# A first FFN block of 256 tokens with attention woven into it, in windowed attention followed by a SwiGLU block

## The chip, the cores and the metric

The kernel runs on one core of a Trainium2 chip. A core has a matrix engine (PE, with its weight loads listed apart as PEld), a vector engine (DVE), a scalar engine (ACT), a general engine (POOL) and a sync engine (SP). Each of the five executes its own instructions in order and waits for the others by semaphores. POOL and SP also issue transfers (DMAs). PE writes only to PSUM, which ACT and DVE then read ("evict") into SBUF. The metric is the device time of one execution in microseconds (us); smaller is better.

## The reference

Attention over 4 batches, 8 heads, 768 tokens and 64 dimensions per head. A token sees the first 4 tokens (the sinks) and the last 128 tokens up to itself. The heads of a token side by side form a row of 512, and 3072 such rows go through a SwiGLU feed-forward block of width 1536.

```python
scores = scale * np.matmul(q, k.transpose(0, 1, 3, 2))
is_sink = pos[None, :] < 4
rel = pos[:, None] - pos[None, :]
in_window = (rel >= 0) & (rel < 128)
a = softmax(np.where(is_sink | in_window, scores, -1e9))
x = (a @ v).transpose(0, 2, 1, 3).reshape(B * S, H * D)
g = x @ w_gate
out = (g * sigmoid(g) * (x @ w_val)) @ w_out
```

## The kernel before

**Groups.** Attention works in 12 groups of 256 tokens, three per batch. Group g needs its own values and the last 128 of the group before it; groups 0, 3, 6 and 9 open a batch and have no earlier window. Its steps are:

- *T* (`step_T`): k and q arrive with tokens in the partitions, and PE transposes them so that the head dimension is there. Each batch has two parts (`PARTS`): part 0 holds its first 512 tokens and takes four T steps, part 1 holds the other 256 and takes two. One step makes eight transposes into one PSUM tile `pt` of the pool `ps_a`, half of it (h = 0) evicted by ACT (L257), the other half (h = 1) by DVE (L259), four copies of 64x256 each, all into one SBUF tile `kqT` per batch.
- *S* (`step_S`, four per group, one per pair of heads): matmuls of scores into `s` (L282, the pool `ps_s` with one buffer), one exp on ACT (L287), one product with the 0/1 mask on DVE (L291).
- *K* (`step_K`): scores against the sinks, for groups that do not open a batch.
- *PV* (`step_PV`, four per group): probabilities times values, with a column of ones for the sum; DVE takes the reciprocal (L331) and scales (L332).
- *X* (`step_X`, two per group): transposes the 128 rows and copies them (L353) into `xT`, the input of an FFN block.

**FFN blocks.** The 3072 rows are cut into blocks, `SIZES = [512, 256, 512, 512, 512, 512, 256]`. A block has 12 gate units (one for 128 columns of the width: four matmuls `pg`, tanh on ACT, four matmuls `pv`, then u and ht on DVE, L386 to L399) and one down unit per 128 rows (12 matmuls `pd`, an ACT copy, a store over SP, L412 to L419). `pg`, `pv` and `pd` share the pool `ps_f` with three buffers.

**Order.** It is written out by hand. `weave(us, slots)` runs the units one after another and hands each unit the attention steps of its slot; a gate unit runs them between `pg` and `pv`. What a step leaves for DVE goes into the list `later`, and `flush()` at the end of the unit emits it, behind the unit's own u and ht. The evictions of T are not put off in this way: they are emitted inside the step, so ahead of u. `pro` runs steps without FFN and emits one put-off item at a time. Before the first gate, T of part 0 and all of groups 0 and 1 run through `pro`. Then come nine gates of block 0 (512 tokens: groups 0 and 1), then T of part 1 and all of group 2 alone (`alone`, slot 9), then nine gates of block 1 (256 tokens: group 2), the other gates of both, and six down units with groups 3 and 4 in the slots. Blocks 2, 3 and 4 hold two groups each by `pair`, blocks 5 and 6 hold group 11.

**Loads.** Nearly all go through POOL's queue, which converts to bf16, in the order of the program: half of the first k and q (two loads of 256 KB), the builds of the identity, of `diag_h` and of the masks on POOL itself, the other half, values of groups 0 and 1 (eight loads each), weights of gate pieces 0 to 3 (`FCH`: the 12 gate units come in pieces of 1, 2, 3, 3 and 3), part 1 of batch 0, and so on. SP loads only `vcf`, the values of the sinks (eight small loads), from which DVE makes `vsb` for all four batches before its first eviction (L205).

Of the kernel before, what the change touches and what calls it, by code (L numbers as in the profile page):

```python
# [15 lines left out]
def kernel(  # L16
# [26 lines left out]
    SIZES = [512, 256, 512, 512, 512, 512, 256]  # L43
# [43 lines left out]
    def load_kq(b, a, k2):  # L87

        t0, r = PARTS[a]
        if k2 == 0:  # L90
            nat[b, a] = natp.tile([P, 2, H, r * D], BF16, tag=f"kq{a}", name="kq")
        hs = slice(4 * k2, 4 * k2 + 4)
        for i, src in ((0, k), (1, q)):
            nc.gpsimd.dma_start(
                nat[b, a][:, i, hs],
                src[b, hs, t0:t0 + r * P].rearrange("h (p r) d -> p h (r d)", r=r))

    def load_v(g):
        b, c = divmod(g, GC)
        va = vpool.tile([P, 2, H, VS], BF16, tag=f"va{g}", name="va")  # L100
        nc.vector.memset(va[:, :, :, D:D + 1], 1.0)
        for j in range(2):
            t0 = c * 256 + j * P
            for r in range(4):
                nc.gpsimd.dma_start(  # L105
                    va[32 * r:32 * (r + 1), j, :, 0:D],
                    v[b, :, t0 + r:t0 + P:4].rearrange("h m d -> m h d"))
        vas[g] = va
# [27 lines left out]

    nc.vector.memset(vcf, 0.0)
    nc.vector.memset(vcf[:, :, D:D + 1], 1.0)
    for h in range(H):
        nc.sync.dma_start(  # L140
            vcf[h * NS:(h + 1) * NS, :, 0:D],
            v[:, h, 0:NS].rearrange("b s d -> s b d"))

    load_kq(0, 0, 0)
    make_identity(nc, ident)
    nc.gpsimd.memset(diag_h, 1.0)
# [8 lines left out]
    def build_masks():  # L155
        nc.gpsimd.memset(mask, 1.0)
        for w in range(4):
            m = mask[32 * w:32 * (w + 1)].rearrange(
                "p a (k r m) -> p a k r m", k=2, r=4)
            nc.gpsimd.affine_select(  # L160
                out=m[:, :, 0], in_=m[:, :, 0], compare_op=ALU.is_gt, fill=0.0,
                base=w, pattern=[[0, 2], [-1, 4], [-4, 32]], channel_multiplier=4)
            nc.gpsimd.affine_select(
                out=m[:, :, 1], in_=m[:, :, 1], compare_op=ALU.is_ge, fill=0.0,
                base=-w, pattern=[[0, 2], [1, 4], [4, 32]], channel_multiplier=-4)

        nc.gpsimd.tensor_copy(out=mask0, in_=mask)
        for w in range(4):
            nc.gpsimd.memset(
                mask0[32 * w:32 * w + 1].rearrange("p a x -> p (a x)")[:, P:3 * P], 1.0)  # L170

    load_kq(0, 0, 1)
    build_masks()
    load_v(0)
    load_v(1)
    for i in range(4):
        load_gate(i)

    def load_b(b):
        for k2 in range(2):  # L180
            load_kq(b, 1, k2)
# [4 lines left out]

    load_b(0)
    load_v(2)
    load_gate(4)
    load_a(1)  # L190
    for i in range(4):
        load_out(i)
    load_v(3)
# [9 lines left out]
    for b in range(B):  # L203
# [7 lines left out]


    kqT, es_t, e_t, xns, xTs = {}, {}, {}, {}, {}
# [7 lines left out]
    def step_T(b, a, n):  # L221
        t0, r = PARTS[a]
        if a == 0 and n == 0:
            kqT[b] = kqtp.tile([P, NP2, 2, S], BF16, tag="kqT", name="kqT")
        ns = r // 2
        pairs = range(n * 2 // ns, (n + 1) * 2 // ns)
        pt = ps_a.tile([P, 2, 4, P], BF16, tag="a", name="pt")
        for h in range(2):
            m = 0
            for p in pairs:  # L230
                for i in range(2):
                    for x in range(ns):
                        nc.tensor.transpose(  # L233
                            pt[:, h, m],
                            nat[b, a][:, i, 2 * p + h, 2 * x * D:2 * (x + 1) * D],
                            ident)
                        m += 1
        for h in range(2):
            for u in range(2):

                src = pt[u * D:(u + 1) * D, h]
                dst = kqT[b][h * D:(h + 1) * D, pairs[0]:pairs[-1] + 1]
                dst = dst.rearrange("q a i s -> q (a i) s")[:, :, t0:t0 + r * P]
                if r == 4:
                    dst = dst.rearrange("q i (t x u m) -> q i x t u m", t=4, x=2, u=2)
                    src = src.rearrange("q (i x) (t m) -> q i x t m", x=2, t=4)
                    for i in range(2):
                        evict(h, dst[:, i, :, :, u], src[:, i])
                else:
                    dst = dst.rearrange("q i (t w u m) -> q i t w u m", t=2, w=2, u=2)  # L250
                    src = src.rearrange("q i (t m w) -> q i t w m", t=2, w=2)
                    for w in range(2):
                        evict(h, dst[:, :, :, w, u], src[:, :, :, w])

    def evict(h, dst, src):
        if h == 0:
            nc.scalar.copy(out=dst, in_=src)  # L257
        else:
            nc.vector.tensor_copy(out=dst, in_=src)  # L259

    def step_ks(b):

        dst = kss[b].rearrange("q (a m) -> q a m", m=KS)
        for h in range(2):
            r = slice(h * D, (h + 1) * D)
            nc.vector.tensor_copy(
                out=dst[r, :, h * NS:(h + 1) * NS], in_=kqT[b][r, :, 0, 0:P:P // NS])

    def step_S(g, p):
# [3 lines left out]
        ps = ps_s.tile([P, 2, 512], FP32, tag="s", name="s")  # L273
        kT, qT = kqT[b][:, p, 0], kqT[b][:, p, 1]
# [4 lines left out]
        for kk, qq, n, col in parts:  # L279
            for h in range(2):  # L280
                r = slice(h * D, (h + 1) * D)
                nc.tensor.matmul(  # L282
                    ps[:, h, col:col + n], kT[r, kk:kk + P], qT[r, qq:qq + n],
# [270 lines left out]
```

## Time and profile before

| | |
|---|---|
| median of 3 runs | 308.81 us (308.06 to 309.0) |
| the profiled execution | 307.91 us, its span 306.2 us |
| PE busy | 258.8 us of the span (85%) |
| DVE busy | 198.2 us (65%) |
| ACT busy | 135.6 us (44%) |
| POOL busy | 98.4 us (32%) |

The profile is of one execution; times in it count from the start of its span. A row of the timeline has the start, the length, the engine, the line of the kernel, the operation, and out<-in with shapes; xN means that N instructions in a row are merged, and the bracket tells how long the engine stood idle before and what ended that. A row of the groups has the busy time and the mean length in ns, and behind the second bar the idle time before them. A row of the waits has the total in us, how often, and the longest. The busy time of PE overstates its work, since matmuls are pipelined.

### The profile page before, as it was taken

To read this page: it belongs to the slowest core of one execution; us is meant where nothing else is said; L and a number is where in the kernel's file an instruction comes from. 1 tells how busy PE (TensorE), PEld (TensorE's weight loads), DVE (VectorE), ACT (ScalarE), POOL (GpSimd) and SP (SyncE) were. 2 spreads that over 40 slices of the span, in tenths; PEclk is the share of its full clock that TensorE was granted. 3 is DMA by queue.
4 is the path that set the end of the run, shared out by engine and by line. 5 is a ranking of instruction groups with operands and counts; after the bars stand their busy time and mean duration, and the time that the engine had idled before them with its cause. 6 is when DMAs were issued, how large, how long until landed. Compare 5 with 4: busy or idle time off the path is not lost.

```text
span 306.2 us, 5085 instructions
## 1 busy us (share of the span) xinstructions
PE 258.8 (85%) x1920; PEld 140.0 (46%) x1920; DVE 198.2 (65%) x462; ACT 135.6 (44%) x261; POOL 98.4 (32%) x165
## 2 busy tenths in 40 slices
PE   0357896588799988889997897999999999999980
PEld 0235443366444543454543444544555445566430
DVE  2766678576876348699546697918997278977000
ACT  1572235526835255844156446436554263333220
POOL 8999376369877244690000000000000000000000
PEclk9999999599999999999999799999999999999996
DMA  7399999999999598692120000022000220000122
GB/s 98 47 58 135 196 111 198 205 83 103 132 79 113 88 158 112 44 102 16 39 81 22 0 2 0 4 70 67 1 0 2 67 72 1 2 0 1 42 89 77
DMA packets 53240, 20.81 MB, mean 68 GB/s; under 512 B 36320, under 2 KB 50144, under 8 KB 53216
## 3 DMA queue, kind: packets, MB, share of 16 engines
q0 software_dynamic: 49888, 14.16, 44.7%
q1 hardware_dynamic: 3328, 6.32, 6.7%
q8 instruction: 15, 0.25, 0.3%
q14 instruction: 9, 0.07, 0.1%
HBM read 28.34 MB, written 6.29 MB: 113 GB/s over the span
## 4 chain that ended last, share of the span: by engine, by line
PE 65%; DVE 16%; ACT 10%; issue 3%; DMA 1%; SPq 1%; DVEq 0%; ACTq 0%
PE pd L412 20%; PE pv L394 16%; PE pg L386 16%; DVE kqT L259 6%; PE s L282 5%; DVE u L398 4%; ACT e L287 4%; ACT kqT L257 4%; PE o L326 4%; PE pt L233 2%; ACT th L389 2%; PE px L350 2%; DVE ht L399 1%; DMA vcf<-in_v_dram 1%; DVE e L291 1%
## 5 line engine op out<-in xcount | busy, mean ns | idle before, releaser
L394 PE MATMUL pv<-xT,wv 128*128 128x512 bf16 (+1 forms) x336 | 76.8, 351 | 10.4 <-DVE u L398 8.5
L389 ACT ACTIVATE th<-pg 128x512 f32<-128x512 f32 (+1 forms) x84 | 45.1, 536 | 87.6 <-PE pg L386 79.2
L386 PE MATMUL pg<-xT,wg 128*128 128x512 bf16 (+1 forms) x336 | 76.8, 351 | 1.6 <-DVE xT L353 1.0
L412 PE MATMUL pd<-wo,ht 128*128 128x512 bf16 x288 | 68.3, 379 | 0.4 <-DVE ht L399 0.4
L398 DVE SCALAR_TENSOR_TENSOR u<-th,pg 128x512 bf16<-128x512 f32 (+1 forms) x84 | 51.2, 610 | 23.7 <-ACT th L389 22.3
L105 POOL DMA_DIRECT2D va<-in_v_dram x96 | 55.8, 619 | 33.1 <-DMA kq<-in_q_dram 11.5
L399 DVE TENSOR_TENSOR ht<-u,pv 128x512 bf16<-128x512 bf16 (+1 forms) x84 | 51.4, 612 | 9.5 <-PE pv L394 1.0
L287 ACT ACTIVATE e<-s 128x1024 bf16<-128x1024 f32 (+1 forms) x48 | 45.6, 950 | 13.2 <-PE s L282 13.0
L386 PEld LDWEIGHTS <-wg 128*128 128x128 bf16 x336 | 32.9, 98 | 33.3 <-issue 3.5
L394 PEld LDWEIGHTS <-wv 128*128 128x128 bf16 x336 | 30.5, 97 | 34.5 <-issue 16.4
L259 DVE COPY kqT<-pt 64x256 bf16<-64x256 bf16 x96 | 27.9, 330 | 19.7 <-ACT kqT L257 16.7
L412 PEld LDWEIGHTS <-ht 128*128 128x128 bf16 x288 | 26.2, 98 | 27.5 <-issue 1.0
L291 DVE TENSOR_TENSOR e<-e,mask 128x1024 bf16<-128x1024 bf16 (+1 forms) x48 | 30.8, 642 | 11.0 <-ACT e L287 10.8
L257 ACT COPY kqT<-pt 64x256 bf16<-64x256 bf16 x96 | 30.5, 367 | 15.9 <-PE pt L233 15.4
L416 ACT ACTIVATE ot<-pd 128x512 f32<-128x512 f32 x24 | 14.3, 597 | 44.3 <-PE pd L412 44.2
L282 PE MATMUL s<-kqT 64*128 64x128 bf16 (+1 forms) x256 | 21.0, 263 | 15.4 <-ACT e L287 10.4
L233 PE MATMUL pt<-ident,kq 128*128 128x128 bf16 x192 | 16.2, 234 | 9.2 <-DMA kq<-in_k_dram 5.9
L282 PEld LDWEIGHTS <-kqT 64*128 64x128 bf16 x256 | 9.4, 100 | 30.5 <-issue 24.1
L326 PEld LDWEIGHTS <-e 128*128 128x128 bf16 x352 | 19.3, 107 | 7.4 <-DVE xn L332 0.8
L332 DVE TENSOR_TENSOR xn<-o,rcp 128x256 bf16<-128x256 f32 x48 | 20.4, 424 | 1.7
L326 PE MATMUL o<-va,e 128*128 128x65 bf16 x352 | 20.9, 207 | 0.7 <-DVE xn L332 0.7
L233 PEld LDWEIGHTS <-kq 128*128 128x128 bf16 x192 | 13.0, 105 | 12.7 <-DMA kq<-in_k_dram 5.9
(35 smaller groups left out, 115.3 us busy)
## 6 DMA issues: line engine op xcount, KB each, us to landing
out_dram<-ot SPq DMA_DIRECT2D x24, 256.0 KB
va<-in_v_dram POOLq DMA_DIRECT2D x96, 32.0 KB, 2.6
kq<-in_k_dram POOLq DMA_DIRECT2D x8, 256.0 KB, 7.1
kq<-in_q_dram POOLq DMA_DIRECT2D x8, 256.0 KB, 8.0
wo<-in_moe_w_out_dram POOLq DMA_DIRECT2D x4, 384.0 KB, 12.6
wg<-in_moe_w_gate_dram POOLq DMA_DIRECT2D x3, 384.0 KB, 7.4
wv<-in_moe_w_val_dram POOLq DMA_DIRECT2D x3, 384.0 KB, 8.6
kq<-in_k_dram POOLq DMA_DIRECT2D x8, 128.0 KB, 3.7
```

What stands on the lines that cost most here:

```text
L105: nc.gpsimd.dma_start(va[32 * r:32 * (r + 1), j, :, 0:D], v[b, :, t0 + r:t0 + P:4].rearrange("h m d -> m h d"))
L257: nc.scalar.copy(out=dst, in_=src)
L259: nc.vector.tensor_copy(out=dst, in_=src)
L282: nc.tensor.matmul(ps[:, h, col:col + n], kT[r, kk:kk + P], qT[r, qq:qq + n], start=True, stop=True)
L287: nc.scalar.activation(e, ps[:, :, lo:512], AF.Exp, scale=scale)
L326: nc.tensor.matmul(o, l, r, start=(i == 0), stop=(i == len(mms) - 1), skip_group_check=True)
L386: nc.tensor.matmul(pg, wgs[fi][:, c, fs], x[:, c, 0:n], start=(c == 0), stop=(c == DMC - 1))
L389: nc.scalar.activation(th, pg, AF.Tanh, scale=0.5)
L394: nc.tensor.matmul(pv, wvs[fi][:, c, fs], x[:, c, 0:n], start=(c == 0), stop=(c == DMC - 1))
L398: nc.vector.scalar_tensor_tensor(u, th, 1.0, pg, op0=ALU.add, op1=ALU.mult)
L399: nc.vector.tensor_tensor(hts[tb][:, f, 0:n], u, pv, op=ALU.mult)
L412: nc.tensor.matmul(po, hts[tb][:, f, ts * P:(ts + 1) * P], wos[f // n][:, f % n], start=(f == 0), stop=(f == DFC - 1))
```

## The change

Five things change together.

1. The blocks become `[256, 512, 512, 512, 512, 512, 256]`. Only group 0 runs ahead of the first gate. Groups 1 and 2, the T steps of part 1 and K of both go into the slots of block 0, which has 14 units; groups 3 and 4 with T of batch 1 go into block 1 by `pair(3, 4, 2)`. Ahead of the first gate every second S step (`wide`) uses two tiles of `ps_f` and two exps, so that it need not wait for `s`.
2. A T step now serves one head of two pairs (part 0) or of four pairs (part 1). K lies in one half of `pt` and is evicted by ACT into a tile `kT`; Q lies in the other and is evicted by DVE into a tile `qT`; two copies of 64x512 each. Within the FFN the Q copies go into `later`, so behind u and ht.
3. The values of group 0 are loaded in fp32 over SP, ahead of `vcf`, into two tiles of the output pool, and DVE casts them (`cast_v`).
4. The masks are built by DVE compares from two index tiles that POOL makes (`iota`); the identity and `diag_h` are cleared by DVE. `vsb` of a batch is made after its fourth T step.
5. The loads on POOL are reordered: weights of gate pieces 0 and 1 come right behind the first k and q, and w_out ahead of batch 1. A load of part 1 covers all heads and half the partitions, with a token order that lets the eviction read without a stride.

```diff
-    SIZES = [512, 256, 512, 512, 512, 512, 256]
+    SIZES = [256, 512, 512, 512, 512, 512, 256]
...
+            else:
+                for w in range(2):
+                    nc.gpsimd.dma_start(
+                        nat[b, a][64 * w:64 * (w + 1), i],
+                        src[b, :, t0:t0 + r * P].rearrange(
+                            "h (n w u) d -> w n h (u d)", w=2, u=2)[w])
...
+    v32 = [opool.tile([P, DM], FP32, tag="ot", name="v32") for _ in range(2)]
+    for j in range(2):
+        for r in range(4):
+            nc.sync.dma_start(
+                v32[j][32 * r:32 * (r + 1)].rearrange("p (h d) -> p h d", d=D),
+                v_src(0, j, r))
...
+    nc.gpsimd.iota(tq, [[1, 4], [4, 32]], base=0, channel_multiplier=0,
+                   allow_small_or_imprecise_dtypes=True)
+    for w in range(4):
+        nc.gpsimd.iota(tk[32 * w:32 * (w + 1)], [[0, 1]], base=w,
+                       channel_multiplier=4, allow_small_or_imprecise_dtypes=True)
...
+        for j in range(2):
+            nc.vector.tensor_scalar(mask[:, j, 0:P], tq, tk, None, op0=ALU.is_lt)
+            nc.vector.tensor_scalar(mask[:, j, P:2 * P], tq, tk, None, op0=ALU.is_ge)
...
-    load_kq(0, 0, 1)
-    build_masks()
-    load_v(0)
-    load_v(1)
-    for i in range(4):
-        load_gate(i)
+    va0 = new_v(0)
+    load_gate(0)
+    load_gate(1)
+    load_v(1)
+    load_gate(2)
+    load_kq(0, 1, 0)
+    load_gate(3)
+    load_gate(4)
+    load_v(2)
...
+        def evict(i):
+            dst = (kTs if i == 0 else qTs)[b][
+                h * D:(h + 1) * D, pairs[0]:pairs[-1] + 1, t0:t0 + r * P].rearrange(
+                "q a (x u m) -> q a x u m", u=2, m=32)
             for u in range(2):
+                d = dst[:, :, :, u]
+                src = pt[u * D:(u + 1) * D, i].rearrange(
+                    "q (a x m) -> q a x m", a=len(pairs), m=32)
+                if i == 0:
+                    nc.scalar.copy(out=d, in_=src)
                 else:
+                    nc.vector.tensor_copy(out=d, in_=src)
+        evict(0)
+        if now:
+            evict(1)
         else:
+            later.append(lambda: evict(1))
...
+                later.append(lambda: build_vsb(b))
...
+    T0, S0, V0, X0 = Ta(0, True), Ss(0), PVs(0), Xs(0)
+    pro(T0[0], T0[1], S0[0], A(step_S, 0, 1, True), T0[2], T0[3], S0[2],
+        A(step_S, 0, 3, True), cast_v)
     flush()
+    pro(*V0)
+    flush()
+    pro(*X0)
     flush()
...
+    v1, x1, v2, x2 = PVs(1), Xs(1), PVs(2), Xs(2)
+    add(sl, *zip((0, 1, 2, 3), Ss(1)), (1, A(step_K, 1)), (4, v1[0]), (4, v1[1]),
+        (5, v1[2]), (5, v1[3]), *zip((5, 6), Tb(0)), *zip((6, 7), x1),
+        *zip((7, 8, 9, 10), Ss(2)), (8, A(step_K, 2)), (11, v2[0]), (11, v2[1]),
+        (12, v2[2]), (12, v2[3]), (12, x2[0]), (13, x2[1]))
+    weave(units(0), sl)
...
+    sl = pair(3, 4, 2)
+    for i, t in zip((0, 1, 2, 3), Ta(1)):
+        sl.setdefault(i, []).insert(0, t)
+    weave(units(1), sl)
```

More of the change, by code (lines that the diff above doesn't have):

```diff
@@ L219, in flush, with step_T @@
         later.clear()
[L221 removed]
+    def step_T(b, a, n, now):
         t0, r = PARTS[a]
         if a == 0 and n == 0:
[L224 to L238, printed above, removed]
[L239 to L253 removed]
```

150 lines of the change are left out of this document (72 added, 78 removed).

## The prediction

> **What bounds the kernel now.** I read the windows first, cut where the FFN blocks begin, then the start, then the waits of the later blocks.
>
> ```profile
> span 306.2 us, 5085 instructions
> 0.00:33.30 33.30, 15.71 (x153) 11.00 (x154) 20.13 (x64) 13.93 (x26) 29.90 (x56) 1.00 0.85 93
> 33.30:48.90 15.60, 15.60 (x74) 7.09 (x74) 11.12 (x17) 5.38 (x9) 10.63 (x17) 1.00 1.32 156
> 48.90:63.90 15.00, 8.19 (x89) 5.70 (x88) 10.29 (x25) 6.97 (x13) 5.45 (x9) 0.66 1.40 192
> 63.90:109.20 45.30, 41.84 (x345) 24.86 (x345) 28.94 (x78) 21.70 (x45) 33.35 (x54) 1.00 0.96 97
> 109.20:155.40 46.20, 41.50 (x314) 21.37 (x312) 33.66 (x79) 23.65 (x49) 19.07 (x31) 1.00 0.66 78
> 155.40:205.10 49.70, 44.55 (x338) 22.98 (x336) 33.91 (x78) 25.16 (x50) 0.00 (x0) 0.97 0.07 21
> 205.10:244.40 39.30, 39.05 (x282) 18.94 (x280) 28.90 (x60) 18.93 (x33) 0.00 (x0) 1.00 0.10 28
> 244.40:306.20 61.80, 52.34 (x336) 28.09 (x334) 31.29 (x62) 19.89 (x36) 0.00 (x0) 0.96 0.11 36
> ```
>
> Columns: stretch, its length, busy PE, PEld, DVE, ACT, POOL, then clock, DMA share, GB/s. PE is the bound wherever FFN runs: 15.60 of 15.60 in the first gates, 39.05 of 39.30 in block 4. It isn't in two stretches of attention alone: up to 33.30 (15.71 busy) and 48.90 to 63.90 (8.19 of 15.00, at clock 0.66). Blocks 2 and 3 lose 4.7 and 5.15 us.
>
> The start:
>
> ```profile
> 7.41 1.68 PE L233 MATMUL pt<-ident,kq 128*128 128x128 bf16 x14 [1.12 <-DMA kq<-in_q_dram]
> 7.85 3.24 DVE L205 TENSOR_TENSOR vsb<-vcf,diag_h 128x520 bf16<-128x520 f32 x4 [4.94 <-DMA vcf<-in_v_dram]
> ...
> 15.26 0.50 PE L282 MATMUL s<-kqT 64*128 64x256 bf16 x4 [1.11 <-ACT e L287]
> ...
> 16.76 1.28 ACT L257 COPY kqT<-pt 64x256 bf16<-64x256 bf16 x4 [0.16 <-PE pt L233]
> 17.20 1.03 PE L233 MATMUL pt<-ident,kq 128*128 128x128 bf16 x8
> 18.08 1.00 DVE L259 COPY kqT<-pt 64x256 bf16<-64x256 bf16 x4 [2.15 <-ACT kqT L257]
> ...
> 33.28 1.02 PE L386 MATMUL pg<-xT,wg 128*128 128x512 bf16 x4 [0.52 <-DVE xT L353]
> ```
>
> The first q lands at 7.4, the first gate starts at 33.28: 25.9 us for attention of groups 0 and 1. DVE's evictions begin behind 3.24 us of vsb, and always when ACT's four copies of the same pt are over (16.76 + 1.28, then 18.08).
>
> The later blocks:
>
> ```profile
> PE pv L394 <- DVE u L398: 8.5, 8, 2.1
> ```
> ```profile
> 111.92 1.53 DVE L259 COPY kqT<-pt 64x256 bf16<-64x256 bf16 x4 [3.10 <-ACT kqT L257]
> ...
> 113.46 0.69 DVE L398 SCALAR_TENSOR_TENSOR u<-th,pg 128x512 bf16<-128x512 f32 x1
> 114.20 1.02 PE L394 MATMUL pv<-xT,wv 128*128 128x512 bf16 x4 [1.51 <-DVE u L398]
> ```
> ```profile
> 119.48 0.68 DVE L291 TENSOR_TENSOR e<-e,mask 128x1024 bf16<-128x1024 bf16 x1
> 119.90 1.02 ACT L287 ACTIVATE e<-s 128x1024 bf16<-128x1024 f32 x1
> ```
>
> DVE is in order. Its copy waits for ACT's, u waits behind that copy, pv finds no free PSUM buffer and PE stands: 8.5 us over the kernel.
>
> **The change, part by part.** Durations that I use:
>
> ```profile
> L353 DVE COPY xT<-px 128x512 bf16<-128x512 bf16 x24 | 10.0, 419 | 8.1 <-PE px L350 8.1
> L398 DVE SCALAR_TENSOR_TENSOR u<-th,pg 128x256 bf16<-128x256 f32 x24 | 10.1, 421 | 3.2 <-ACT th L389 3.2
> L399 DVE TENSOR_TENSOR ht<-u,pv 128x256 bf16<-128x256 bf16 x24 | 10.1, 421 | 2.5
> L291 DVE TENSOR_TENSOR e<-e,mask 128x1024 bf16<-128x1024 bf16 x32 | 22.0, 687 | 9.8 <-ACT e L287 9.7
> L291 DVE TENSOR_TENSOR e<-e,mask 128x768 bf16<-128x768 bf16 x16 | 8.9, 553 | 1.2 <-ACT e L287 1.2
> L332 DVE TENSOR_TENSOR xn<-o,rcp 128x256 bf16<-128x256 f32 x48 | 20.4, 424 | 1.7
> L331 DVE RECIPROCAL rcp<-o 128x4 f32<-128x4 f32 x48 | 8.5, 177 | 4.4 <-PE o L326 4.0
> ```
> ```profile
> L416 ACT ACTIVATE ot<-pd 128x512 f32<-128x512 f32 x24 | 14.3, 597 | 44.3 <-PE pd L412 44.2
> L287 ACT ACTIVATE e<-s 128x768 bf16<-128x768 f32 x16 | 12.9, 808 | 3.2 <-PE s L282 3.1
> ```
> ```profile
> 54.71 1.02 ACT L287 ACTIVATE e<-s 128x1024 bf16<-128x1024 f32 x1 [0.70 <-PE s L282]
> 56.43 1.02 ACT L287 ACTIVATE e<-s 128x1024 bf16<-128x1024 f32 x1 [0.70 <-PE s L282]
> ```
>
> *Evictions.* Four copies of 64x512 replace eight of 64x256 per step. Nearest rows: 419 ns on DVE (same width, from PSUM), 597 on ACT. So K costs 1.2 us (1.28 before), Q 0.85 (1.00 to 1.53). Do the two now run side by side? Two tiles in SBUF suggest it. But ACT writes e at 119.90 while DVE still works on another part of e, so sharing an SBUF tile does not order them; what the two copies also share is pt in PSUM, and they still do. I take K then Q in series; side by side is a rival.
>
> The Trainium skill ("PSUM — Partial Sum Buffer", "PSUM bank collisions raise a hardware error") says that two engines must be kept apart on one bank and 32-partition quadrant, reads against reads included. It speaks against this part of the change, and the rows at 16.76 and 18.08 agree; by the rule the start has the serial sum below, without it 1.7 us less.
>
> *Values over SP, and the loads.*
>
> ```profile
> 1.25 2.75 SPq L140 DMA_DIRECT2D vcf<-in_v_dram  x8
> ...
> 285.02 13.54 SPq L418 DMA_DIRECT2D out_dram<-ot  x6
> ```
> ```profile
> 3.69 4.04 DMA vcf<-in_v_dram
> ```
> ```profile
> 13.42 9.20 POOL L105 DMA_DIRECT2D va<-in_v_dram  x16
> ```
> ```profile
> 32.00:40.00 8.00, 7.23 (x38) 3.27 (x36) 5.30 (x9) 2.27 (x4) 2.60 (x5) 1.00 1.45 195
> ```
>
> Eight loads of 256 pieces (32 rows, 8 heads) go ahead of vcf on SP. The POOL row shows pieces of that kind at 4096 in 9.20 us, 445 per us; so 2048 take 4.6 us, landing near 10. No row shows SP's queue that fast: its stores move 128 pieces per 2.6 us (paced by their matmuls), which is the far bound, 42 us. I take the near one, since the DMA engines are the same and a store's piece is 2 KB. The pieces fall among the first k and q; half of 2048 ahead of q would be 2.3 us, spread over both loads I take 1.2: q at 8.6 (bounds 7.4 and 12). vcf follows, issued by about 9 and landing 4 later, 13; vsb wants it near 19.
>
> POOL loses the masks and eight value loads: weights start after four loads of k and q and a few small builds, near 7 instead of 22.5. By the end of w_out 6.8 MB are due (k, q 1.0 and 0.5, gates 3.1, two value groups 0.5, w_out 1.6, and roundings); at the row's 195 GB/s 35 us, plus 3 for the start and 4.6 for the SP pieces: 42.5, wanted near 51 (below). Hidden, with 8 us of cover. At 156 GB/s (second window) it is 51: no cover left. The k and q of part 1 come in four loads as before, each now for half the partitions, of the same pieces; I cost that at nothing, as they are wanted 10 us after the first gate. The loads of batch 1 stand behind w_out, 1.0 MB or 5 us more, and are wanted at the end of block 0, near 59; block 0's two stores share the engines then.
>
> Masks on DVE: four compares of 128 columns, a copy and four small memsets, 1.5 us at rows like 419 ns; they end near 8, before DVE has Q to evict (10.5). If POOL's new index builds take 2 us longer, it is still covered.
>
> *The start, from q's landing.* Half a step's transposes at the 1.03 of eight, and 0.2 until ACT sees them: first eviction at 0.7. K 1.2, K 1.2, Q 0.85 (the first Q lies beside the second K): 3.95. S 0.5 plus 0.25 to be seen, exp 0.81, the wide step's two half exps, together 1.0: 6.5. Two more K, then Q 0.85: 9.75. S, exp and half exps again: 12.3. Two masks of 0.55: 13.4. Four normalisations of 0.60 (424 + 177): 15.8. Transposes of xn and the copies 0.42 each, the first beside the second's transposes: 17.1. First gate at 8.6 + 17.1 = 25.7, where it was 33.28, though group 1 is still to do. At nothing I cost the first mask, the step for ks, vsb of batch 0 (a quarter of 3.24) and the two casts of values (0.42 each): DVE does them between Q at 9.75 and the mask at 12.4, 2.65 us for some 2.6. Without that cover each adds its length.
>
> *Block 0, 256 tokens, 12 gates and 2 downs, groups 1 and 2 inside.* A unit with S repeats at 1.73 (54.71, 56.43), as exp and S alternate over one PSUM tile; DVE's u, ht, mask are 1.53, so that chain sets it. Units 0 to 3: 6.9, and 0.4 to start. Units 4 to 7: DVE sets them: four gates 3.4, four PV 2.4, two Q 1.7, two xT 0.84, a mask 0.69: 9.0. Units 8 to 10: 5.2; both K steps 0.4. Unit 11: 2.0. Two downs of 2.6 with PV and X between: 6.7. Together 30.6. The clock adds: 8 transposes take 1.03 at 17.20, so PE may enter at its slow rate; about 1.5. Waits between engines 0.9. Block 0: 33, ends at 58.7. Bounds: DVE's own sum, 24 (12 gates 10.1, masks 5.5, PV 4.8, Q and xT 3.4), and 39, if each of the four-unit stretches loses 2 to 3.
>
> *Block 1, 512 tokens, T(1), groups 3 and 4.* Block 2 has the same work plus two T steps, 41.50 of PE. I take 41 and 1.5 of waits: 42.5, to 101.2. Before, this point was 109.2.
>
> *Blocks 2 to 4.* The Q copy now comes after u and ht, so u no longer stands behind ACT. PE's 41.50 + 44.55 + 39.05 = 125.1; less 1.5, because block 3's clock of 0.97 over 49.7 us is a dip that its idle time goes with; plus 3 of new waits: S in the unit after a T step now waits for a Q copy queued behind u, ht and perhaps a mask. 126.6, was 135.2. Bounds 124 and 135. Blocks 5 and 6 keep 61.8.
>
> *Sum.* 25.7 + 33 + 42.5 + 126.6 + 61.8 = 289.6 of span, was 306.2. The profiled execution took 307.91, 1.7 more than its span: 291.3. The median of the runs is 0.9 above it: **292**.
>
> **Rivals.**
> (1) *More gain*: evictions side by side (1.7 at the start) and block 0 nearer DVE's sum (3 less): 287.5. For it: two tiles. Against: the copies at 18.08.
> (2) *The deferral only moves the stall*: S after T waits as pv did, blocks 2 to 4 keep 135.2 and block 1 loses 2 more: 303. For it: the same DVE work stands in one queue. Against: in the row at 114.20 pv waited because u stood behind the copy; with u ahead only S waits, and four pg matmuls and a T step run on PE before it.
> (3) *Weights late*: at 140 GB/s instead of 195, w_out comes near 56, 5 late: 297. For it: the first window moved 93. Against: that one was held by value loads issued singly.
> (4) *Slower*: SP's queue makes its pieces one at a time. At the store's pace the values land at 43; PV of group 0 wanted them at 21. All else before it is done, so the start moves 22: 314. It decides from a landing at 37.5, where the 16.5 of gain are spent. vcf's own pace, 128 pieces from 1.25 to 7.73, would be far worse, 100 us. Against: its eight transfers hold only 16 pieces each, and most of that time is one latency of 4.04.
>
> The Trainium skill ("DMA: Bandwidth & Descriptors", "Issuing engines are not separate DMA queues") says that all queues run on the same 16 DMA engines and a second issuer saves only issue time; by that the values cost q what they bring, as the 1.2 above has it, and rival 4 does not occur.
>
> **How the numbers follow.** Forecast 0.62, (1) 0.13, (2) 0.10, (3) 0.07, (4) 0.08. 0.3% (0.9 us) is about what a measurement of this kernel can tell from no change. Forecast and rivals 1 to 3 are all faster by more: 0.91 with a little of 4; slower 0.07; the same 0.02. The range 283 to 304 takes in rivals 1 to 3 and block 0's bounds; the forecast's own is 287 to 297.
>
> **What would show it.** First gate near 26 and first q near 8.6; the cast of values not waiting for its DMA; DVE's copy of Q starting as ACT's of K ends in the start, after ht later; "pv waits for u" below 3 us and some "s waits for qT"; block 0 of about 33 with DVE over 70% busy; pd not waiting for wo. Wrong if the first gate is past 30, the values land after 21, or blocks 2 to 4 keep over 131.

## The result and the profile after

The changed kernel took 287.53 us as the median of 4 runs (287.39 to 287.94), where the kernel before took 308.73 (308.06 to 309.0): a ratio of 0.9319, 95% interval 0.9301 to 0.9337. The forecast was 292.0 in a range of 283 to 304, so the sign and the size hold, and 4.5 us of gain were missing in it. The profiled execution took 287.39 with a span of 285.7.

The windows of the changed kernel, cut where its FFN blocks begin (stretch, length, busy PE, PEld, DVE, ACT, POOL, clock, DMA share, GB/s):

```profile
0.00:24.30 24.30, 9.58 (x80) 6.65 (x81) 14.72 (x52) 8.94 (x15) 18.94 (x37) 1.00 1.13 143
24.30:54.00 29.70, 27.17 (x281) 18.74 (x281) 21.66 (x57) 15.86 (x27) 15.43 (x24) 1.00 1.33 172
54.00:95.30 41.30, 40.09 (x297) 20.36 (x296) 30.34 (x65) 21.04 (x33) 33.37 (x55) 1.00 1.15 110
95.30:138.40 43.10, 41.07 (x314) 21.18 (x313) 32.43 (x68) 23.33 (x37) 17.93 (x30) 1.00 0.69 82
138.40:182.70 44.30, 42.52 (x338) 22.36 (x337) 32.51 (x67) 24.42 (x38) 0.00 (x0) 1.00 0.08 23
182.70:221.40 38.70, 38.70 (x282) 19.12 (x281) 27.65 (x56) 18.70 (x29) 0.00 (x0) 1.00 0.10 28
221.40:285.70 64.30, 52.48 (x337) 28.16 (x335) 31.31 (x62) 19.88 (x36) 0.00 (x0) 0.93 0.12 36
```

Against the stretches before, the first gate comes 9.0 us earlier (24.3, was 33.3). By the start of block 2, when the same groups are done, the lead is 13.9 (95.3, was 109.2), and by the start of block 5 it is 23.0 (221.4, was 244.4). The last stretch gives back 2.5 (64.3, was 61.8), although its matmuls are the same.

PE's waits in the changed kernel, first over the whole span, then from block 1 to block 4 alone (total, times, longest):

```profile
PE s L315 <- DVE qT L282: 8.4, 9, 1.6
...
PE o L363 <- DVE va L495: 1.3, 1, 1.3
```

```profile
PE s L315 <- DVE qT L282: 3.0, 4, 1.0
...
PE pv L432 <- DVE u L436: 0.3, 1, 0.3
```

The wait of 8.5 us for u is down to 0.3, and a new one stands beside it, S waiting for the Q copy, 3.0 us in blocks 1 to 4 and 5.4 ahead of them (4.4 in the start, 1.0 in block 0).

The start in time order:

```profile
8.35 1.46 PE L265 MATMUL pt<-ident,kq 128*128 128x128 bf16 x12 [1.50 <-DMA kq<-in_q_dram]
8.99 2.36 ACT L280 COPY kT<-pt 64x512 bf16<-64x512 bf16 x4 [6.91 <-PE pt L265]
10.20 0.85 DVE L282 COPY qT<-pt 64x512 bf16<-64x512 bf16 x2 [1.63 <-ACT kT L280]
11.39 0.86 DVE L282 COPY qT<-pt 64x512 bf16<-64x512 bf16 x2 [0.34 <-ACT kT L280]
...
24.32 1.01 PE L424 MATMUL pg<-xT,wg 128*128 128x256 bf16 x4 [0.52 <-DVE xT L390]
```

The Q copy of each step starts when ACT has finished the K copies of the same step, as the prediction took it: K first (two copies, 1.2 us), then Q, in series.

### The profile page after: what moved, and what is told of

It reads as the page before. It is cut to its first block, busy times and chain, and to the rows that moved or that the text cites. A ratio compares the mean times of both kernels' runs of the same rounds, so it can differ in the third digit from the quotient of the medians.

```text
span 285.7 us, 4989 instructions
## 1 busy us (share of the span) xinstructions
PE 251.6 (88%) x1920; PEld 136.6 (48%) x1920; DVE 190.6 (67%) x427; ACT 132.2 (46%) x215; POOL 85.7 (30%) x146
## 4 chain that ended last, share of the span: by engine, by line
PE 68%; DVE 11%; DMA 8%; ACT 4%; POOL 3%; issue 2%; DVEq 0%; POOLq 0%; ACTq 0%
PE pd L450 22%; PE pv L432 18%; PE pg L424 16%; DMA wv<-in_moe_w_val_dram 5%; PE s L315 4%; PE o L363 3%; DMA va<-in_v_dram 3%; DVE qT L282 3%; DVE ht L437 3%; DVE u L436 3%; ACT th L427 2%; PE px L387 2%; PE pk L338 1%; PE pt L265 1%; POOL kq L97 1%
## 5 line engine op out<-in xcount | busy, mean ns | idle before, releaser
L123 POOL DMA_DIRECT2D va<-in_v_dram x88 | 50.8, 598 | 30.9 <-DMA kq<-in_q_dram 9.1
L324 ACT ACTIVATE e<-s 128x1024 bf16<-128x1024 f32 (+1 forms) x46 | 43.9, 955 | 8.2 <-PE s L315 7.8
L432 PEld LDWEIGHTS <-wv 128*128 128x128 bf16 x336 | 28.8, 98 | 21.9 <-issue 6.2
L454 ACT ACTIVATE ot<-pd 128x512 f32<-128x512 f32 x24 | 14.3, 597 | 52.5 <-PE pd L450 52.4
L280 ACT COPY kT<-pt 64x512 bf16<-64x512 bf16 x48 | 27.8, 579 | 17.0 <-PE pt L265 11.8
L328 DVE TENSOR_TENSOR e<-e,mask 128x1024 bf16<-128x1024 bf16 (+1 forms) x48 | 30.7, 640 | 1.5 <-ACT e L324 1.4
L315 PE MATMUL s<-qT,kT 64*128 64x128 bf16 (+1 forms) x248 | 19.8, 245 | 9.0 <-DVE qT L282 8.4
L282 DVE COPY qT<-pt 64x512 bf16<-64x512 bf16 x48 | 20.1, 420 | 6.1 <-ACT kT L280 5.6
L363 PEld LDWEIGHTS <-e 128*128 128x128 bf16 x352 | 17.4, 100 | 8.7 <-issue 1.7
L315 PEld LDWEIGHTS <-kT 64*128 64x128 bf16 x256 | 8.8, 96 | 24.2 <-issue 18.2
L265 PE MATMUL pt<-ident,kq 128*128 128x128 bf16 x128 | 11.3, 242 | 9.3 <-DMA kq<-in_k_dram 6.2
L390 DVE COPY xT<-px 128x512 bf16<-128x512 bf16 x24 | 10.1, 421 | 9.8 <-PE px L387 9.7
```

What stands on the lines that cost most here:

```text
L123: nc.gpsimd.dma_start(va[32 * r:32 * (r + 1), j, :, 0:D], v_src(g, j, r))
L282: nc.vector.tensor_copy(out=d, in_=src)
L315: nc.tensor.matmul(pss[h][:, col:col + n], kT[r, kk:kk + P], qT[r, qq:qq + n], start=True, stop=True)
L324: nc.scalar.activation(e, ps[:, :, lo:512], AF.Exp, scale=scale)
L328: nc.vector.tensor_tensor(e, e, m[:, :, lo:512].broadcast_to([P, 2, 512 - lo]), op=ALU.mult)
L363: nc.tensor.matmul(o, l, r, start=(i == 0), stop=(i == len(mms) - 1), skip_group_check=True)
```

## The experiments

Where nothing else is said, an experiment is the changed kernel with one edit. The ratio is to the kernel before on the same chip. A difference in us is one of medians from different chips, on which the kernel before took 307.4 to 309.0; reckoned by the ratios it would come out up to 1 us otherwise. Of each run one execution was traced. The time after the last matmul varies by up to 2.5 us among the traces with whole stores (8.8 to 11.3), so differences of 1 or 2 us are read block by block, from the first tanh of one block to that of the next.

**The Q copies back into their T step.**

```diff
-        if now:
+        if True:
             evict(1)
```

> The changed kernel with every Q copy put back into its own T step, ahead of the exponentials' products u on DVE; the two tiles, the order and the loads stay. My theory: the deferred copies are what removed the 8.5 us of waits of PE for u in blocks 1 to 4; with the copies back in front, u stands behind a Q copy that itself waits for ACT's K copies, and blocks 1 to 4 together grow from 167.4 by 4 to 6 us, start and block 0 the same: 291 to 294. Rival: with two tiles and K on ACT alone the DVE queue is short enough, and deferring only moves where a stall is counted: 287 to 288.5.

Measured: 292.78 us (292.0 to 293.42), ratio 0.9498 (0.9441 to 0.9555), 5.2 us more than the changed kernel. PE's waits over the span, and the place in block 1:

```profile
PE pv L432 <- DVE u L436: 6.5, 11, 1.3
...
PE s L315 <- DVE qT L282: 4.4, 4, 1.6
```
```profile
59.68 0.86 DVE L282 COPY qT<-pt 64x512 bf16<-64x512 bf16 x2 [3.42 <-ACT kT L280]
60.55 0.69 DVE L436 SCALAR_TENSOR_TENSOR u<-th,pg 128x512 bf16<-128x512 f32 x1
...
61.29 1.02 PE L432 MATMUL pv<-xT,wv 128*128 128x512 bf16 x4 [0.71 <-DVE u L436]
```

The wait for u is back, by the path that the prediction described: DVE stands 3.42 us until ACT has copied K, then copies Q, and only then makes the u that pv's buffer hangs on. S waits 4.0 less in exchange. From tanh to tanh, block 0 grew by 2.9 us (29.6 to 32.6), blocks 1 to 3 by 4.1 together and block 4 not at all; the last stretch was 1.0 shorter. I had expected block 0 unchanged, so the size fits and its spread does not. In block 0, 1.1 of the 2.9 is a clock that rose later (last section). The rest stands at the T steps, where PE waits for Q copies and the granted clock, third from the end of the row, then falls to half for 3.4 us:

```profile
36.30:40.30 4.00, 2.09 (x24) 1.67 (x25) 1.95 (x6) 2.03 (x4) 3.52 (x5) 1.00 0.50 48
40.30:43.70 3.40, 3.09 (x22) 2.16 (x21) 3.08 (x10) 1.06 (x3) 3.40 (x6) 0.50 1.21 194
```

The changed kernel has no such fall in its blocks. The second rival of the prediction, that putting the copy off only moves the stall, is refuted.

**A PSUM tile of its own for Q in the start.**

```diff
+        pts = [pt, pt]
+        if now:
+            pts[1] = ps_f.tile([P, 2, 512], BF16, tag="f", name="ptq")
...
-                src = pt[u * D:(u + 1) * D, i].rearrange(
+                src = pts[i][u * D:(u + 1) * D, i].rearrange(
```

> The changed kernel, where in the T steps that run before the first gate the transposes of Q are written to a PSUM tile of their own; the rest as it is. My theory: in the start DVE's Q copy begins where ACT's K copy of the same step ends because both read one PSUM tile; with a tile for each, the Q copies of the first T steps begin when their transposes are done, the first gate comes 1 to 2.5 us earlier than 24.3, and the time is 285 to 286.5. Rival: the Q copies are late for another reason (PE's order of the transposes, the landing of q at 8.3), their starts stay, and the time is 287.2 to 287.9.

Measured: 285.44 us (285.03 to 285.77), ratio 0.9257 (0.9195 to 0.9319), 2.1 below the changed kernel. Its start:

```profile
12.62 2.37 ACT L284 COPY kT<-pt 64x512 bf16<-64x512 bf16 x4
12.74 1.75 DVE L286 COPY qT<-ptq 64x512 bf16<-64x512 bf16 x4 [0.17 <-PE ptq L269]
...
21.17 1.01 PE L428 MATMUL pg<-xT,wg 128*128 128x256 bf16 x4 [0.52 <-DVE xT L394]
```

Now the K and Q copies run side by side, and DVE waits for PE's transposes and no longer for ACT. It was the shared tile in PSUM, and not the destination, that put them in series. The first gate comes 3.15 us earlier, of which 1.6 were lost again in block 0, 0.9 of it in a wait of pd for w_out, with whose landings the earlier start had caught up. The 3.15 is from one trace. A later run with the same start (tile and split stores together) has its first gate at 22.35, 2.0 earlier than the changed kernel: its first k landed 0.6 later, and DVE waited 0.95 us there for vcf, the values of the sinks, where it waited 0.19 in the trace above and not at all in the changed kernel.

The Trainium skill ("PSUM — Partial Sum Buffer", "PSUM bank collisions raise a hardware error") has two engines on the same bank and 32-partition quadrant kept apart, two reads as well; these two traces agree, with the copies in series out of one tile and side by side out of two.

**The new copies alone, in the kernel before.** Two tiles, K by ACT, Q by DVE and put off (in batch 0 at once), with the part-1 loads that belong to them; block sizes, order, the other loads and masks as before.

```diff
...
-        pt = ps_a.tile([P, 2, 4, P], BF16, tag="a", name="pt")
+        h = n % 2
+        pairs = range(NP2) if a else range(n // 2 * 2, n // 2 * 2 + 2)
+        pt = ps_a.tile([P, 2, 512], BF16, tag="a", name="pt")
...
+        evict(0)
+        if now:
+            evict(1)
+        else:
+            later.append(lambda: evict(1))
...
```

> The kernel before with the new copies alone: K and Q to two tiles, K by ACT, Q by DVE, the Q copy deferred behind the step after; the block sizes, the order of the start, the loads and the masks as before. My theory: the waits for u in blocks 1 to 4 go, and some 8 to 9.5 of the 21.2 us come from here: 299 to 301; the other 12 come from the block of 256 at the front and the loads. Rival: the copies are worth little without the new order (the wait turns up elsewhere), 304 to 308, and the order carries nearly all.

Measured: 300.66 us (299.19 to 302.27), ratio 0.9756 (0.969 to 0.9822); on 308.7 that is 7.5 us, with an interval of 5.5 to 9.6. The time is within what I expected, and the gain just under the 8 to 9.5. Its stretches:

```profile
0.00:35.40 35.40, 16.34 (x152) 11.11 (x153) 19.48 (x56) 13.59 (x18) 30.07 (x56) 1.00 0.87 97
...
154.30:198.60 44.30, 42.09 (x331) 22.37 (x336) 31.92 (x66) 24.43 (x38) 0.00 (x0) 1.00 0.08 23
198.60:237.30 38.70, 38.44 (x276) 19.11 (x280) 27.67 (x56) 18.70 (x29) 0.00 (x0) 1.00 0.10 30
```

Blocks 3 and 4 have the lengths of the changed kernel (44.3, 38.7), so what they gained is the copies' work alone. In the kernel before, block 3 (49.7) also held 3.4 us of half clock, from 168.4 on, right behind a wait of pv for u of 2.07; that is gone here too. The start is 2.1 us longer than before (35.4, was 33.3); S waits 5.3 us for qT in it, where it waited 2.7 for kqT.

**The old copies in the changed kernel**, with the part-1 loads that belong to them; the reverse of the run above.

```diff
...
-            kTs[b] = kqtp.tile([P, NP2, S], BF16, tag="kT", name="kT")
-            qTs[b] = kqtp.tile([P, NP2, S], BF16, tag="qT", name="qT")
+            kqT[b] = kqtp.tile([P, NP2, 2, S], BF16, tag="kqT", name="kqT")
+            kTs[b], qTs[b] = kqT[b][:, :, 0], kqT[b][:, :, 1]
...
```

> The changed kernel with the copies and the part-1 loads of the kernel before: K and Q in one tile, the copies of a T step shared out between ACT and DVE by head and made at once; order, masks and first values stay as changed. The reverse of the run with the new copies alone, which took 8.1 us off. My theory: block order and copies act on different stretches, the new copies on the waits for u in blocks 1 to 4 (6 to 8.5 us), the order on the start and on block 0, so the loss here is about the same, less what the old copies save in the start, where they run on two engines at once (1 to 2.5 us): 293 to 295.5. Rival: the new order has put the T steps where their copies no longer hold up u, and the old copies cost little: 288 to 291.

Measured: 300.2 us (298.7 to 302.84), ratio 0.9718 (0.9641 to 0.9795). That is 12.7 more than the changed kernel; I had expected 5.5 to 8, and the rival less. PE's wait for u:

```profile
PE pv L425 <- DVE u L429: 11.3, 12, 2.1
```

And block 0 in this run:

```profile
37.61 1.29 ACT L278 COPY kqT<-pt 64x256 bf16<-64x256 bf16 x4 [1.55 <-PE pt L254]
38.93 1.53 DVE L280 COPY kqT<-pt 64x256 bf16<-64x256 bf16 x4 [2.11 <-ACT kqT L278]
40.61 0.82 PE L254 MATMUL pt<-ident,kq 128*128 128x128 bf16 x8 [2.16 <-DVE kqT L280]
```

So the two gains are not a sum. Alone the copies bring 7.5 us and the rest 8.7 (0.9718 of 308.7), together 21.2: 5.0 of it needs both, give or take some 3 by the intervals of the ratios. Which part of the rest carries the 8.7 was not separated further than by the runs on values and masks below. In the trace, whose span is 13.9 longer, 7.9 of the loss stands in blocks 2 to 4, 3.3 in block 0, 2.1 in block 1 and 0.8 in the start, where I had expected the old copies to save a little. The new order puts the T steps of part 1, which ran alone before, into gates of block 0, where the old copies hold DVE for ACT's 2.11 and their own 1.53, and PE's next transposes for 2.16 (row at 40.61). Block 0 takes 33.0 where it took 29.7. About 1 of that is the clock that rose later; the rest includes 3.4 us of half clock from 40.8 on, behind that wait, and how much each costs was not separated. The T steps of batch 1 now stand in the first gates of block 1: the wait for u is 3.2 there, where the kernel before has 0.8 in its first two blocks. The old order, for its part, let the new copies cost 2.1 in the start.

**The first values over POOL, as before.**

```diff
...
-    va0 = new_v(0)
+    load_v(0)
     load_gate(0)
...
-        A(step_S, 0, 3, True), cast_v)
+        A(step_S, 0, 3, True))
```

> The changed kernel with the first values loaded as before, by eight issues on POOL's queue ahead of the weights and cast on the way, not over SP and cast by DVE. My theory: POOL holds eight transfers at a time, so the weights move back by the 3 to 5 us that these eight take, w_out lands 3 to 5 us later than 42.4 to 48.5 and its cover of some 1 us is gone; pd waits 2 to 4 us in block 0, the start itself gains up to 0.9 for an earlier q or a cast less: 288.5 to 291. Rival: the weights have slack, where the first values go is worth nothing, 287 to 288.

Measured: 288.86 us (287.71 to 289.11), ratio 0.9378 (0.933 to 0.9426), some 1.3 more. The time is what my theory said, and the trace has both halves larger than that. PE's start, and pd in block 0:

```profile
7.39 1.46 PE L259 MATMUL pt<-ident,kq 128*128 128x128 bf16 x12 [0.92 <-DMA kq<-in_q_dram]
...
48.61 0.81 PE L444 MATMUL pd<-wo,ht 128*128 128x512 bf16 x3 [0.92 <-DMA wo<-in_moe_w_out_dram]
50.88 1.14 PE L444 MATMUL pd<-wo,ht 128*128 128x512 bf16 x3 [1.11 <-DMA wo<-in_moe_w_out_dram]
52.90 2.94 PE L444 MATMUL pd<-wo,ht 128*128 128x512 bf16 x9 [0.45 <-DMA wo<-in_moe_w_out_dram]
```

q lands 0.96 earlier without SP's eight loads beside it, and the first gate comes at 22.60, 1.7 earlier. Then pd starts each of the last three quarters of its sum when the next piece of w_out lands: the trace's DMA records have the four pieces at 46.42, 48.56, 50.84 and 52.86. In the changed kernel they landed at 42.38, 44.45, 46.42 and 48.54. These waits are 2.5 us, yet block 0 is 5.0 longer from tanh to tanh: 0.6 is the clock that rose later, and most of the other 1.9 lies where the clock falls to half behind the waits, as the nine pd matmuls in 2.94 us show (2.11 in the changed kernel):

```profile
51.20:54.60 3.40, 2.95 (x12) 1.21 (x10) 0.42 (x1) 0.23 (x1) 1.20 (x3) 0.50 1.38 199
```

So 1.7 gained and 5.0 lost would be 3.3; the last stretch happened to be 1.5 shorter in this execution.

**The masks on POOL, as before, ahead of the first weights.**

```diff
+        nc.gpsimd.memset(mask, 1.0)
+        for w in range(4):
+...
-            nc.vector.tensor_scalar(mask[:, j, 0:P], tq, tk, None, op0=ALU.is_lt)
```

> The changed kernel with the masks built as before by POOL, ahead of the issues of the first weights. My theory: POOL's issues stand still while it builds them, all weights come 5 to 8 us later, the first gate is late only if the first weights come after 24.3 (they landed at 13 to 17, so it is not), but pd waits for w_out 4 to 7 us at the end of block 0: 291 to 295. Rival: DVE is relieved of some 7 us of memsets and compares in the start and the first gate comes earlier, so that it comes out even: 286 to 288.

Measured: 287.16 us (286.49 to 288.24), ratio 0.9333 (0.9284 to 0.9382): no difference that these runs can tell. My theory is wrong on the time. (In the trace this run is 1.2 us behind at the first tanh of block 5, 1.0 of it from the clock that rose later, and has a last stretch that is 2.1 shorter.) POOL's first weight is issued 5.2 us later (11.40 against 6.23), but the queue makes up part of it, and w_out lands 2.8 to 3.2 later, the last piece at 51.49. pd meets it with hardly a wait; its last two quarters in this run, then in the changed kernel:

```profile
50.35 0.81 PE L449 MATMUL pd<-wo,ht 128*128 128x512 bf16 x3
51.53 2.10 PE L449 MATMUL pd<-wo,ht 128*128 128x512 bf16 x9
```
```profile
49.62 0.81 PE L450 MATMUL pd<-wo,ht 128*128 128x512 bf16 x3
50.49 2.11 PE L450 MATMUL pd<-wo,ht 128*128 128x512 bf16 x9
```

The last quarter begins just behind that landing, 1.18 after the third where it is 0.87 in the changed kernel: 0.3 lost. There the last piece, at 48.54, led its use at 50.49 by 2 us; here block 0 began its gates at the full clock 1 us later, and lead and delay together cover the 3 us. That DVE gains from the relief, as the rival had it, does not show: the first gate is at 24.1, 0.2 earlier. In the changed kernel DVE's compares and memsets end at 8.6, and its first copy of Q waits for ACT until 10.20; here it waits until 10.28.

**Both of these together.**

> The changed kernel with both the masks built by POOL ahead of the weights and the first values over POOL. Each alone moved w_out's landings by 3 to 4.3 us and used up the 2 us by which the last of them had led pd. My theory: together they move it by 7 to 8, pd then waits 5 to 6 us in block 0, q's earlier landing gives back 1.7: 290.5 to 292.5. Rival: the first value loads and the masks overlap on POOL (the eight places are taken by k and q meanwhile), the two shifts don't add, and the time is that of the values alone, 288 to 289.5.

Measured: 291.98 us (291.1 to 294.11), ratio 0.9434 (0.9371 to 0.9496), 4.5 above the changed kernel, with the last w_out at 57.29. Beside w_out the gate weights are late too (pg waits 1.89 for the one, pd 0.95 to 1.15 for three quarters and 0.20 for the last):

```profile
31.44 0.61 PE L417 MATMUL pg<-xT,wg 128*128 128x256 bf16 x4 [1.89 <-DMA wg<-in_moe_w_gate_dram]
...
57.33 2.69 PE L443 MATMUL pd<-wo,ht 128*128 128x512 bf16 x9 [0.20 <-DMA wo<-in_moe_w_out_dram]
```

The granted clock was 0.51 from 55.1 to 58.5, behind these waits, and nine pd matmuls took 2.69 us. So each of the two moves was nearly free to leave out (1.3 us and none), and both together are worth 4.5 us: block 0 has one reserve, and either of them may spend it.

**Each store split into four.**

```diff
-        nc.sync.dma_start(
-            out[r0:r0 + P].rearrange("(m r) d -> r m d", r=4), ot)
+        for r in range(4):
+            nc.sync.dma_start(
+                out[r0 + r:r0 + P:4], ot[32 * r:32 * (r + 1)])
```

> The changed kernel with each store of a block of 128 tokens split into four, one for each residue of the row; the same bytes in the same pieces. My theory: the 11.2 us from the last matmul to the last landing are set by stores that use 4 of the 16 DMA engines each; split, the pieces spread over more engines, the last landing comes 3 to 6 us earlier, and the time is 281.5 to 284.5, everything ahead of the last matmul the same. Rival: each of the four still goes to few engines or the issues on SP take what is gained: 287 to 289.

Measured: 281.66 us (281.49 to 282.1), ratio 0.9141 (0.9089 to 0.9192), 5.9 below the changed kernel. Blocks 5 and 6 up to the last matmul, and what follows, in the kernel before, in the changed kernel and here:

```profile
244.20:297.30 53.10, 52.53 (x337) 28.18 (x335) 31.29 (x62) 19.30 (x35) 0.00 (x0) 1.00 0.09 29
297.30:306.20 8.90, 0.01 (x1) 0.00 (x0) 0.00 (x0) 0.60 (x1) 0.00 (x0) 0.74 0.21 80
```
```profile
221.40:274.40 53.00, 52.43 (x337) 28.16 (x335) 31.31 (x62) 19.28 (x35) 0.00 (x0) 1.00 0.10 28
274.40:285.70 11.30, 0.04 (x1) 0.00 (x0) 0.00 (x0) 0.60 (x1) 0.00 (x0) 0.60 0.22 71
```
```profile
222.10:275.30 53.20, 52.31 (x333) 28.16 (x335) 31.33 (x62) 19.29 (x35) 0.00 (x0) 1.00 0.13 32
275.30:279.90 4.60, 0.00 (x0) 0.00 (x0) 0.00 (x0) 0.60 (x1) 0.00 (x0) 0.90 0.31 76
```

The matmuls take 53 us in all three; only what comes after the last one differs: 8.9, 11.3 and 4.6. Cut more closely to the time in which the stores run:

```profile
263.60:274.40 10.80, 10.80 (x51) 4.70 (x48) 0.00 (x0) 2.39 (x4) 0.00 (x0) 1.00 0.25 71
274.40:284.60 10.20, 0.04 (x1) 0.00 (x0) 0.00 (x0) 0.60 (x1) 0.00 (x0) 0.62 0.24 79
```
```profile
264.40:275.20 10.80, 10.75 (x50) 4.67 (x48) 0.00 (x0) 2.39 (x4) 0.00 (x0) 1.00 0.43 102
```

A DMA share of 0.25 is four of sixteen engines, and it stays there as long as stores run; split, it is 0.43, near seven on average. Six stores of 128 pieces of 2 KB had been queueing on four engines since 11 us before the last matmul.

The Trainium skill ("DMA: Bandwidth & Descriptors", "Why a DMA increments its semaphore by 16 and not by 1") lets a transfer that SP issues use the largest number of engines, up to 16, that divides the slowest dimension of both sides; the whole store's destination is 4 by 32 rows, and the share of four engines agrees.

**Tile and split stores together; then the loads interleaved; then the values over POOL again.** The second of the three adds this to the first:

```diff
...
-    load_v(1)
+    load_v(1, (0,))
     load_gate(2)
+    load_v(1, (1,))
     load_kq(0, 1, 0)
     load_gate(3)
+    load_v(2, (0,))
     load_gate(4)
-    load_v(2)
+    load_v(2, (1,))
```

> Both the PSUM tile of its own for Q in the start and the split stores. My theory: the two gains lie at the two ends and add up, 281.7 less 2.1 is 279.6; 279 to 280.2. Rival: the trace of the tile's run shows w_out landing after PE asks for it (0.9 us), so what the start gains is partly given back in block 0 also here, and with another order of landings it can be given back whole: 281 to 282.

> As the run with both, and the small value loads of groups 1 and 2 are issued half before and half behind a weight pair (four, gate 2, four; gate 3, four, gate 4, four), where they were eight in a row. My theory: eight small transfers in a row fill the eight places of POOL's queue and the DMA engines run dry while they are handed out again (36 to 40 us: 48 GB/s, against 185 to 203 around it), so w_out comes 2 to 4 us earlier, pd no longer waits, and the time falls by 0.7 to 1.5 below the run with both: 278 to 279. Rival: the bytes, not the places, set when w_out lands, and the order changes nothing: within 0.4 of the run with both.

> As the run with both gains and the interleaved loads, and the first values over POOL behind the first weight pair instead of over SP. My theory: SP's eight value loads share the DMA engines with the first k and q, without them q lands 0.9 us earlier and the casts on DVE go (the trace with the values on POOL had its first gate 1.7 us earlier); the interleaving left w_out some 4 us of lead, which takes up the 2 to 4 us by which the weights move back: 276.5 to 277.8. Rival: the weights move back by more than the lead and pd waits again, or the values come too late for the first PV: 278.3 to 280.

Measured: 278.72 us (278.35 to 279.78), ratio 0.9052 (0.9001 to 0.9102); 278.30 (278.08 to 278.59), ratio 0.9043 (0.9001 to 0.9085); 278.14 (277.53 to 278.27), ratio 0.9009 (0.8955 to 0.9063). The two gains add up: 8.8 us below the changed kernel, 2.1 and 5.9 would be 8.0. The other two steps are within what these runs can tell. Yet the second did what it was made for. POOL has eight loads under way at a time: in the changed kernel its twelfth is issued at 12.55, as the fourth lands, and its fourteenth at 14.15, as the sixth lands. The stretch from 36 to 40 in the first run of the three, then in the second:

```profile
36.00:40.00 4.00, 2.53 (x31) 1.95 (x32) 3.75 (x12) 2.06 (x5) 3.22 (x5) 1.00 0.58 46
```
```profile
36.00:40.00 4.00, 2.84 (x32) 1.95 (x31) 3.61 (x10) 2.42 (x5) 3.74 (x6) 1.00 1.24 207
```

46 GB/s became 207, and the last of w_out landed at 43.55 where it had been 48.96. But pd did not wait for w_out in the first run of the three either, so 5.4 us of earlier landing bought nothing. In the third the first gate came 0.6 earlier than in the second (20.78 against 21.37), not 1.7 as in the run with the shared tile. Its q landed 0.78 earlier (7.39 against 8.17), but DVE was still building masks until 8.59, so its first Q copy began at 8.62 where it had begun at 8.81: in this start the masks on DVE are no longer hidden.

## Why the prediction was right, point by point

- *First gate, 25.7*: 24.3. q landed at 8.3 (forecast 8.6), and from there the start took 16.0 (forecast 17.1). K before Q in series was right, and the run with two PSUM tiles shows why. The first rival's half of this, copies side by side, did not occur, and was worth 3.15 and 2.0 us of start in the two traces where it was made to occur; the prediction had priced it at 1.7.
- *Values over SP, near 10, and cost 1.2 of q*: q lost 0.96 by the run without them, and the first PV waited 1.3 for DVE's cast, not for a transfer. The casts, with three other items, had been put at nothing, as DVE would have time for them; they did not fit in whole, and this 1.3 is what was left. The fourth rival, SP's queue piece by piece, is gone. The rule cited with it from the Trainium skill ("DMA: Bandwidth & Descriptors", "Issuing engines are not separate DMA queues"), that all queues share the same DMA engines, agrees with these 0.96.
- *w_out at 42.5, 8 us of cover*: the weakest step. 42.4 was the first of four pieces; the last came at 48.5, and led its use by 2 us. The sum by 195 GB/s missed the lulls: 36 to 40 ran at 48 GB/s, when eight small value loads in a row filled the places of POOL's queue. With them interleaved, w_out is at 43.6, near the forecast. The mistake cost nothing, since the lead held; that the lead would be 2 us and not 8 was not foreseen.
- *Block 0, 33*: 29.7, the largest miss of a term (3.3). The mis-sized row is the repeat of a unit with S, read as 1.73 from two exps at 54.71 and 56.43, at a time of clock 0.66. In block 0 after:

```profile
29.81 1.02 ACT L324 ACTIVATE e<-s 128x1024 bf16<-128x1024 f32 x1
31.32 1.02 ACT L324 ACTIVATE e<-s 128x1024 bf16<-128x1024 f32 x1 [0.15 <-PE s L315]
```

  The repeat is 1.51, ACT idles 0.15 between exps instead of 0.70. Seven such units are 1.5 us: the slow clock was in that row already, and 1.5 had been put on for it besides (it cost some 1, in the first two units). The rest, some 1.4, is spread over units 8 to 10, the downs and the 0.9 of waits. Units 4 to 7, set by DVE, took 9.6 from exp to exp (31.32 to 40.92), forecast 9.0. DVE was busy for 21.66 of 29.70, 73%, as forecast.
- *Block 1, 42.5*: 41.3. *Blocks 2 to 4, 126.6*: 126.1. PE's sum in them is 122.3 of 126.1, so PE is busy for 97% of them. The wait for u went from 8.5 to 0.3 over the whole kernel; the new wait of S came to 2.0 in blocks 2 to 4, for which 3 had been put down, and to 3.0 with block 1. The 1.5 taken off for block 3's clock was right: it reads 1.00 there now.
- *Blocks 5 and 6 kept at 61.8*: 64.3. The matmul part is unchanged; the tail is 2.4 longer. I had taken the tail for a constant. It is the end of a queue of stores whose pieces took 98 ns each on average in the trace of before and 109 in this one (768 pieces on four engines: 18.9 us and 20.9). The median piece took 84 ns in both. The difference is a few slow pieces: 21 over 300 ns in the one and 36 in the other, together 11.0 and 18.4 us, up to 0.9 us each. In the nine traces with whole stores the tail lies between 8.8 and 11.3, in the four with split ones, where no piece took over 180 ns, it is 4.6. Why some pieces are slow stays open.
- *The first rival, 287.5*: the time fell on its number, by half of its reasons. Block 0 was the 3 us shorter that it says, the copies did not run side by side.
- *Sum*: the start was 1.4 shorter, block 0 3.3, block 1 1.2, blocks 2 to 4 0.5, the tail 2.5 longer: 3.9 less of span. The other 0.6 is that the profiled execution here is within 0.1 of the median, where I added 0.9, less 0.2 of rounding. Part of the closeness is luck: without the longer tail, which no term had, the forecast would have been 7 us too high. The chances of the cases that are faster add up to 0.92, not 0.91.
- *Masks on DVE, nothing*: right, by the run with the masks on POOL; nothing is what they bring alone, too. Together with the values it is different, as the run without both shows.

What the sum could not show is that its parts need each other: 7.5 us from the copies alone, 8.7 from everything else alone, 21.2 from both (a gap of 5.0, give or take 3).

## What to carry to other kernels

An engine that runs in order passes on the wait of whatever stands at its head: an eviction that has to wait for another engine belongs behind the work that the bound engine is waiting for, and here that alone is worth 5.2 us, with what the clock loses behind such waits. A wait that vanishes in a trace shows what it was worth only in the order in which it stood: test a part in the old surroundings and in the new ones, since the two differed here by some 5 us. Look at the stretch after the last matmul by itself, with the DMA share beside it; a share that stands at a quarter says that the transfer's shape, not the amount, sets the end.

## What was not expected of the hardware

The clock at which PE enters the FFN differs between executions of the same start. The third group of four pv matmuls, in the changed kernel and in the one with split stores, which are the same up to there:

```profile
28.40 0.60 PE L432 MATMUL pv<-xT,wv 128*128 128x256 bf16 x4
```
```profile
28.95 1.03 PE L432 MATMUL pv<-xT,wv 128*128 128x256 bf16 x4
29.80 0.62 PE L424 MATMUL pg<-xT,wg 128*128 128x256 bf16 x4
```

Four matmuls of 256 take 1.03 us until the full rate is granted and 0.60 after it. (The clock records of the two traces begin at 27.6 and 29.8; before that the clock column of the windows reads 1.00 without a record.) It came at 27.6 in the one and at 29.8 in the other, and block 0 took 29.6 in the one and 30.7 in the other. A microsecond of difference in the first block between two edits is therefore no evidence for either.

A wait of PE may cost more than its length. In seven places between the first gate and the last matmul the granted clock reads 0.50 or 0.51 for 3.4 or 10.2 us. Two are in the kernel before, at 52.4 and 168.4; one each is in the runs with the Q copies back, the copies alone, the old copies, the values on POOL, and values and masks on POOL. In the 4 us or so ahead of each, PE was busy for about half of the time: 2.09 of 4.30 and 2.33 of 4.40 in the kernel before, 1.73 to 2.09 of 4.00 in the others. The changed kernel's leanest 4 us in its blocks are 2.34 busy, and its clock stays at 1.00 there. That is no complete rule: 4 us as lean as 1.1 (from 29.4 with values and masks on POOL) and 2.0 (from 157.1 with the old copies) were not followed by a fall. What decides it is open.
